# Scoring keys 16384 at a time in a decode attention kernel, with shared PE weights, longer DMA rows and a new split of the load buffers

## The chip, the cores and the metric

The kernel runs on one core of one Trainium2 chip. The time is device microseconds from launch to end, as the median of several executions. The span in a profile is counted from the first to the last instruction and is about 1.7 us shorter than the time. The profile names the engines PE (matmul), PEld (its weight loads), DVE (vector), ACT (scalar), POOL and SP (which issues the bulk loads). PEclk is the share of full speed that the PE clock is granted.

All runs used here are of the state that the measurement calls fast.

## The reference, cut to what matters

```python
def _A_ref(x, k_cache, v_cache, wq, wo):          # one token: attention over a cache
    q = (x @ wq)...                               # 32 heads of 128
    k = jnp.repeat(k_cache, 8, axis=1)            # 4 groups x 65536 keys x 128, bf16
    v = jnp.repeat(v_cache, 8, axis=1)
    p = _softmax(jnp.einsum('bhqd,bhkd->bhqk', q, k) * Dh ** (-0.5))
    return jnp.einsum('bhqk,bhkd->bhqd', p, v)... @ wo

def _B_ref(x, w_in, w_sp, b_sp, w_out):           # a gated mixer on the same token
    ...
return g * a + (1 - g) * b                        # g = sigmoid(sum(x * gate_w))
```

The two caches are 64 MB each (67.1 million bytes), the weights some 28 million bytes. In all 162.0 million bytes must be read from HBM for one token. There is little arithmetic per byte.

## The kernel before: the parts that matter

K and V come in pieces of 8192 keys, and one load brings a pair of them. The loads of K, V and the weights form one list, `stream`. SP issues the list in order on one queue, and load n goes to slot n % 5 of a ring of five slots of 32 KB per partition:

```python
NS = 5; SLOT = 16384                              # elements of 2 bytes
def kv(cache, n):                                 # two pieces: 32 KB per partition
    g, u = KV[n]
    return cache[0, g, UK * u:UK * (u + 2), :].rearrange("(p x) d -> p (x d)", p=128)

def issue(upto):
    while issued[0] < min(upto, len(stream)):
        n = issued[0]
        assert n < NS or all(k in used for k in stream[n - NS][0])
        ...
        P("SP", f, w=[("slot", s)], dma="s%d" % s)      # f: dma_start into slot n
```

A K piece is transposed by DVE in four quarters and scored by PE, four matmuls to a quarter, each with its own weights. Its scores are moved from PSUM by DVE (`score_piece`), exponentiated by ACT, transposed by DVE, and multiplied with V in four column groups of PE:

```python
def k_piece(n, j):
    ...
    P("DVE", lambda e: e.transpose(ktb(i).bitcast(F32), sl[:, 2048 * j:2048 * (j + 1)].bitcast(F32)), ...)
    def f(e):
        for fe in range(4):
            ...
            ins = e.matmul(pf(sb), qpad[g % 2][:, o:o + 128], vw(ktb(i), ...), ...)

def pv_piece(n):
    def f(e):
        for b in range(16):
            cg = b % 4
            ins = e.matmul(pf(OB)[32 * cg:32 * (cg + 1), :], ptsb(n)[:, 32 * b:32 * (b + 1)],
                           vw(sl, 128 * b, [[2048, 4], [1, 128]]), ..., tile_position=(0, 32 * cg), ...)
    P("PE", f, r=[("ptsb", n % 2), key], w=[B(OB)])
    done(("v", n))                                 # the slot may be loaded again
```

Of the kernel before, what the change touches and what calls it, by code (L numbers as in the profile page):

```python
# [137 lines left out]
def bass_gated_mix__gqa_block_cached__mixer_gmlp__decode_kernel(  # L138
# [25 lines left out]
    TILES = 64  # L164
    UK = 128 * TILES
    NU = Sk // UK
    NS = 5
    SLOT = 16384
    QP = 152
    NKTS = 3  # L170
    NSC = 10
    QW = DO // 4
    SCALE = 1.0 / math.sqrt(Dh)
# [3 lines left out]
    assert Sk % UK == 0 and FC == 14 and OC == 32 and HG == 8  # L177
# [4 lines left out]
    def region(name, nbf):  # L182
        nonlocal cur
        OFF[name] = cur
        cur += (nbf + 31) // 32 * 32

    for name, n in [
        ("RING", NS * SLOT), ("KT", NKTS * 2048), ("SC", NSC * 1024), ("PSB", 1024), ("PTSB", 1024),
        ("QPAD", 2 * 4 * QP), ("IDB", 128), ("IDF", 256), ("BM", 256), ("ONES", 256), ("SEL", 16 * 32),
        ("M16", 32), ("M8", 16), ("M32", 64), ("MQ", 32), ("OT", 256), ("XT", KC), ("WB", 2), ("WBB", 4), ("ONEB", 128), ("MAXC", 2 * G * NU), ("LP", 2 * G * NU),  # L190
        ("COLS", 2 * 64), ("DM", 32), ("QT", 32), ("QALL", 128), ("XW", 3 * KC), ("OSC", 512), ("OV", OC), ("Z", 2 * 28), ("Z2", 2 * 28),
        ("ZG", 2 * 28), ("ZE", 2 * 28), ("YB", FC), ("BROW", 2 * QW), ("OROW", QW),
    ]:
        region(name, n)
# [14 lines left out]
    idb, idf, bm, ones = ab("IDB", 128), af("IDF", 128), af("BM", 128), af("ONES", 128)  # L209
    sel, m16, m8 = ab("SEL", 512), af("M16", 16), af("M8", 8)  # L210
    m32, mq, ot = af("M32", 32), af("MQ", 16), af("OT", 128)
    xT, wb, wbb, oneb = ab("XT", KC), ab("WB", 2), af("WBB", 2), ab("ONEB", 128)
    qpad = [ab("QPAD", 4 * QP, 4 * QP * i) for i in range(2)]
    qall = ab("QALL", 128)
    maxc, lp, colt = af("MAXC", G * NU), af("LP", G * NU), af("COLS", 64)
    zc, z2, zg, ze = af("Z", 28), af("Z2", 28), af("ZG", 28), af("ZE", 28)
    yb, ovec, orow, brow = ab("YB", FC), ab("OV", OC), ab("OROW", QW), af("BROW", QW)
    osc, dm = ab("OSC", 512), af("DM", 16)
    qsb, qT, xw = ab("PSB", 512), ab("QT", 32), ab("XW", 3 * KC)
# [4 lines left out]
    def gcol(g, i):  # L224
        return col(C_G4 + 11 * g + i)

    (K_M, K_NB, K_MH, K_L, K_RL, K_F) = range(6)

    def slot(n):
        return ab("RING", SLOT, (n % NS) * SLOT)  # L230

    ktb = lambda i: ab("KT", 2048, (i % NKTS) * 2048)
    scs = lambda n: af("SC", 512, (n % NSC) * 512)
    psb = lambda i: ab("PSB", 512, 512 * (i % 2))
    ptsb = lambda i: ab("PTSB", 512, 512 * (i % 2))

    bank = [nc.alloc_psum_tensor("pb%d" % i, [128, 512], F32) for i in range(8)]
    FB, PTB, OB, MB = 0, 5, 6, 7
    SCB = [3, 4]
    pf = lambda i: bank[i][:, :]  # L240
    pbf = lambda i: bank[i][:, :].bitcast(BF16)
# [4 lines left out]
    def B(i):  # L246
        return ("bank", i)


    P("POOL", lambda e: e.memset(idf, 0.0), w=["idf"])  # L250
# [3 lines left out]
    for i in range(2):  # L254
        P("POOL", lambda e, i=i: e.memset(qpad[i], 0.0), w=[("qpad", i)])
# [3 lines left out]
    P("DVE", lambda e: e.memset(pf(MB), 0.0), w=[B(MB)])  # L259
    P("DVE", lambda e: e.memset(pf(OB), 0.0), w=[B(OB)])  # L260
    P("DVE", lambda e: e.memset(pf(FB), 0.0), w=[B(FB)])
    P("DVE", lambda e: e.memset(xw, 0.0), w=["xw"])
# [9 lines left out]
    xrow, grow, prod = ab("SC", 512, (NSC - 2) * 1024), ab("SC", 512, (NSC - 3) * 1024), af("SC", 512, (NSC - 4) * 512)  # L272
    KX, KG, KP = [("sc", NSC - i) for i in (2, 3, 4)]
# [10 lines left out]
    def load(keys, pieces):  # L284

        for i, key in enumerate(keys):
            place[key] = (len(stream), i)
        stream.append((keys, pieces))
# [4 lines left out]

    WQ_N = HQ * Dh

    def kv(cache, n):

        g, u = KV[n]
        return cache[0, g, UK * u:UK * (u + 2), :].rearrange("(p x) d -> p (x d)", p=128)

    def pair(name, cache, n):
        load([(name, n), (name, n + 1)], [(0, kv(cache, n))])

    KV = [(g, u) for g in range(G) for u in range(NU)]
    total = G * NU
    for i in range(0, 4, 2):
        load([("wq", i), ("wq", i + 1)], [(0, rows(A_wq, i // 2, 4))])
    steps = []
    for n in range(NU):
        if n % 2 == 0:  # L310
            pair("k", A_k_cache, n)
        aux = ()
        if n in (1, 3):
            load([("win", n - 1), ("win", n)], [(0, rows(B_w_in, n // 2, 4))])
            aux = (("win", n - 1), ("win", n))
        elif n == 5:
            load([("wout", 0), ("wout", 1)], [(0, rows(B_w_out, 0, 14))])
        elif n == 6:
            aux = (("wout", 0), ("wout", 1))
        steps.append((n, None, aux))  # L320
    for n in range(NU, total + NU + 1):
        k = n if n < total else None
        v = n - NU - 1
        if k is not None and k % 2 == 0:
            pair("k", A_k_cache, k)
        if v >= 0:
            if v % 2 == 0:
                pair("v", A_v_cache, v)
        else:
            v = None  # L330
        steps.append((k, v, ()))
    WO = [(0, 0, 8), (1, 0, 8), (2, 0, 8), (3, 0, 4), (3, 4, 6), (3, 6, 8)]
    for i, c0, c1 in WO:
        load([("wo", i, c0)], [(0, rows(A_wo, i, 8)[:, DO * c0:DO * c1])])

    WIDTH = {"wq": 2 * WQ_N, "win": 2 * F, "wout": 7 * DO, "wo": 8 * DO, "k": UK, "v": UK}
    issued = [0]
    used = set()

    def issue(upto):  # L340
        while issued[0] < min(upto, len(stream)):
            n = issued[0]
            assert n < NS or all(k in used for k in stream[n - NS][0])
            keys, pieces = stream[n]
            s = n % NS

            def f(e, n=n, pieces=pieces):
                for c0, src in pieces:
                    ins = e.dma_start(slot(n)[:, c0:c0 + src.shape[1]], src)  # L349
                return ins  # L350
            P("SP", f, w=[("slot", s)], dma="s%d" % s)
            issued[0] += 1

    def use(key):
        n, i = place[key]
        issue(n + 1)
        used.add(key)
        w = WIDTH[key[0]]
        return slot(n)[:, i * w:(i + 1) * w], ("slot", n % NS)

    def done(key):

        n = place[key][0]
        if key == stream[n][0][-1]:
            issue(n + NS + 1)

    issue(NS)
# [9 lines left out]
    P("DVE", lambda e: e.tensor_reduce(mq, vw(idf, 0, [[1, 16], [16, 8]]), AXX, ALU.add), r=["idf"], w=["mq"])  # L377


    sele = ab("SC", 512, (NSC - 1) * 1024)  # L380
    KSE = ("sc", NSC - 1)
# [5 lines left out]

    def f(e):
        for c in range(4):
            ins = e.transpose(pbf(PTB)[:, 2 * c:2 * c + 2], vw(xrow, c, [[4, 128]], 0, 2), idb[0:2, 0:2])  # L390
        return ins
    P("PE", f, r=[KX, "idb"], w=[B(PTB)])
    P("DVE", lambda e: e.tensor_copy(vw(xT, 0, [[4, 2], [1, 4]]), vw(pbf(PTB), 0, [[1, 2], [2, 4]])),
      w=["xT", B(PTB)])
    P("DVE", lambda e: e.tensor_copy(vw(xw, 1, [[3, KC]]), xT), r=["xT"], w=["xw"])
    P("PE", lambda e: e.matmul(pf(MB)[:, 0:2], oneb[0:1, :], wb[0:1, :], start=True, stop=True),  # L396
      r=["oneb", "wsp", "bsp"], w=[B(MB)])
    P("DVE", lambda e: e.tensor_copy(wbb, pf(MB)[:, 0:2]), w=["wbb", B(MB)])  # L398
# [4 lines left out]
    P("PE", lambda e: e.matmul(pf(PTB)[:, 0:1], ones[0:2, :], col(C_GS)[0:2, :], start=True, stop=True),  # L403
      r=["ones", "gs"], w=[B(PTB)])
    P("ACT", lambda e: e.activation(col(C_GE), pf(PTB)[:, 0:1], ACTF.Exp, scale=-1.0), w=["ge", B(PTB)])
# [5 lines left out]
    for i in range(4):  # L411
        sl, key = use(("wq", i))

        def f(e, i=i, sl=sl):
            for k in range(2):
                c = 2 * i + k
                for s in range(2):
                    for cg in range(4):
                        ins = e.matmul(pf(OB)[32 * cg:32 * cg + 2, :], xw[:, 3 * c + 1 - s:3 * c + 3 - s],  # L419
                                       sl[:, WQ_N * k + 512 * (4 * s + cg):WQ_N * k + 512 * (4 * s + cg + 1)],  # L420
                                       start=(c == 0 and s == 0), stop=(c == KC - 1 and s == 1),
                                       tile_position=(0, 32 * cg), skip_group_check=True)
            return ins
        P("PE", f, r=["xw", key], w=[B(OB)])
        done(("wq", i))
# [19 lines left out]



    nbatch = [0]
    pend = []

    def q_piece(g):
# [238 lines left out]
```

## Time and profile before

| | before |
|---|---|
| time | 386.56 us, median of 3 (386.56 to 386.72) |
| load queue busy, share of 16 engines' span | 98.2% |
| PE, DVE busy | 61%, 55% |
| 32 KB packet, median | 1.216 us, which is 16 x 32768 B / 1.216 us = 431 GB/s |
| last load byte | 381.2 us of a 384.9 us span |

From the page of the kernel before come the busy shares, two of the rows over 40 slices of the span (digits are tenths), the load queue (packets, MB, share of 16 engines), the chain of waits, and three groups of instructions (busy us, mean ns, then the idle time before them and what ended it):

```profile
span 384.9 us, 3607 instructions
PE 233.6 (61%) x1547; PEld 86.2 (22%) x1547; DVE 211.6 (55%) x329; ACT 30.6 (8%) x71; POOL 2.1 (1%) x9
...
PEclk9985969569996969696889696956796979866655
DMA  8999999999999999999999999999999999999994
...
q1 hardware_dynamic: 6200, 162.01, 98.2%
...
DMA 71%; PE 16%; DVE 11%; issue 0%; SPq 0%
...
L464 DVE STREAM_TRANSPOSE arena<-arena 128x1024 f32<-128x1024 f32 x128 | 151.4, 1217 | 75.3 <-DMA arena<-in_A_k_cache_dram 75.0
L472 PEld LDWEIGHTS pb<-arena 128*128 128x128 bf16 x512 | 46.7, 109 | 201.3 <-DVE arena L464 144.9
L516 PE MATMUL pb<-arena 128*32 128x512 bf16 x512 | 39.3, 441 | 20.6 <-DMA arena<-in_A_v_cache_dram 18.1
```

The DMA row has a 9 in every slice but the first and the last, so the loads bound the kernel from end to end. DVE waits 75.0 us for K, and PE 18.1 us for V. The weight loads of the scores (L472 PEld) are 46.7 us of work, but PEld waits 144.9 us for DVE before them, so they are not what PE waits for. The PEclk row alternates between 9 and 5 or 6: PE keeps falling idle, and after that runs at half clock for a while (below, after 6.11 us idle).

The timeline of the kernel before has 16 PV matmuls of one piece at full clock, and the last two pieces (32 matmuls) at half clock. Its columns are start us, length us, then the instruction:

```profile
186.41 1.05 PE L516 MATMUL pb<-arena 128*32 128x512 bf16 x16
...
362.18 3.60 PE L516 MATMUL pb<-arena 128*32 128x512 bf16 x32 [6.11 <-DMA arena<-in_A_v_cache_dram]
```

### The profile page before, as it was taken

What the parts mean: (1) busy time and instruction counts of PE and PEld (TensorE: products, weight loads), DVE (VectorE), ACT (ScalarE), POOL (GpSimd) and SP (SyncE); (2) the same over time, 40 slices, a digit from 0 to 9 for tenths busy, and PEclk for the clock granted to TensorE, in tenths of its full rate; (3) what the DMA queues carried; (4) which work ended last, traced back from release to release, by engine and by line L of the source; (5) the groups of instructions that cost most, each with busy time, mean ns of one, the idle gap of its engine ahead of it and who ended that gap; (6) DMA issues with size and microseconds to landing.
All of it is one profiled execution on the core that took longest, in us unless ns stands there. A gap on an engine that the chain in (4) does not pass through costs nothing.

```text
span 384.9 us, 3607 instructions
## 1 busy us (share of the span) xinstructions
PE 233.6 (61%) x1547; PEld 86.2 (22%) x1547; DVE 211.6 (55%) x329; ACT 30.6 (8%) x71; POOL 2.1 (1%) x9
## 2 busy tenths in 40 slices
PE   0434888478776656563687574726983829533354
PEld 0111455423221111111222121212220202211121
DVE  4115454489967474655596656645974748511010
ACT  1000000100300000001010000000100000320000
POOL 2000000000000000000000000000000000000000
PEclk9985969569996969696889696956796979866655
DMA  8999999999999999999999999999999999999994
GB/s 331 436 433 440 430 424 437 429 435 433 427 433 426 427 433 429 433 432 436 433 429 436 424 429 436 429 431 430 433 433 431 433 430 429 434 433 422 421 418 169
DMA packets 6228, 162.24 MB, mean 422 GB/s; under 512 B 700, under 2 KB 708, under 8 KB 964
## 3 DMA queue, kind: packets, MB, share of 16 engines
q1 hardware_dynamic: 6200, 162.01, 98.2%
q8 instruction: 12, 0.20, 0.2%
q14 instruction: 4, 0.03, 0.0%
q10 hardware_dynamic: 12, 0.00, 0.0%
HBM read 162.01 MB, written 0.00 MB: 421 GB/s over the span
## 4 chain that ended last, share of the span: by engine, by line
DMA 71%; PE 16%; DVE 11%; issue 0%; SPq 0%
DMA arena<-in_A_k_cache_dram 59%; PE pb L472 11%; DMA arena<-in_A_v_cache_dram 10%; DVE arena L464 9%; DMA arena<-in_A_wo_dram 3%; PE pb L516 2%; PE pb L558 2%; DVE arena L485 1%; PE pb L650 1%; DVE arena L507 0%; DVE arena L533 0%; PE pb L538 0%; PE pb L528 0%; SPq L349 0%; PE pb L495 0%
## 5 line engine op out<-in xcount | busy, mean ns | idle before, releaser
L472 PE MATMUL pb<-arena 128*128 128x512 bf16 x512 | 160.0, 457 | 93.6 <-DVE arena L464 91.7
L464 DVE STREAM_TRANSPOSE arena<-arena 128x1024 f32<-128x1024 f32 x128 | 151.4, 1217 | 75.3 <-DMA arena<-in_A_k_cache_dram 75.0
L472 PEld LDWEIGHTS pb<-arena 128*128 128x128 bf16 x512 | 46.7, 109 | 201.3 <-DVE arena L464 144.9
L516 PE MATMUL pb<-arena 128*32 128x512 bf16 x512 | 39.3, 441 | 20.6 <-DMA arena<-in_A_v_cache_dram 18.1
L502 ACT ACTIVATE arena<-arena 128x512 bf16<-128x512 f32 x32 | 23.1, 720 | 224.0 <-DVE arena L507 171.1
L507 DVE STREAM_TRANSPOSE arena<-arena 128x512 bf16<-128x512 bf16 x32 | 21.6, 679 | 18.5 <-PE pb L516 18.5
L485 DVE TENSOR_SCALAR_CACHE_REDUCE arena<-pb 128x512 f32<-128x512 f32 x32 | 21.6, 674 | 8.1 <-PE pb L472 7.9
L516 PEld LDWEIGHTS pb<-arena 128*32 128x32 bf16 x512 | 12.8, 106 | 45.0 <-issue 37.1
L558 PEld LDWEIGHTS pb<-arena 128*128 128x128 bf16 x224 | 13.8, 161 | 0.4
L558 PE MATMUL pb<-arena 128*128 128x1 bf16 x224 | 13.7, 198 | 0.0
L650 PE MATMUL pb<-arena 128*1 128x256 bf16 x128 | 7.8, 410 | 6.3 <-DMA arena<-in_A_wo_dram 6.3
L530 DVE RECIPROCAL arena<-pb 128x1 f32<-128x1 f32 x4 | 0.7, 168 | 18.4 <-PE pb L528 18.4
L419 PE MATMUL pb<-arena 128*2 128x512 bf16 x64 | 6.8, 601 | 4.2 <-DMA arena<-in_A_wq_dram 4.2
L656 DVE TENSOR_TENSOR arena<-pb,arena 97x256 bf16<-97x256 f32 x1 | 0.4, 425 | 13.4 <-PE pb L650 13.4
L396 PE MATMUL pb<-arena 1*128 1x2 bf16 x1 | 0.2, 158 | 10.1 <-DMA arena<-in_B_b_sp_dram 10.1
L426 DVE CAST arena<-pb 98x512 bf16<-98x512 f32 x1 | 0.7, 692 | 10.2 <-PE pb L419 10.2
L502 ACT ACTIVATION_READ_ACCUMULATOR arena<-arena 128x1 f32 x32 | 6.0, 187 | 0.0
L650 PEld LDWEIGHTS pb<-arena 128*1 128x1 bf16 x128 | 3.4, 109 | 10.5 <-DMA arena<-in_A_wo_dram 7.6
L538 PE MATMUL pb<-arena 128*128 128x128 bf16 x16 | 1.8, 243 | 5.2 <-DVE arena L533 5.2
L573 ACT ACTIVATE arena<-arena 128x28 f32<-128x28 f32 x1 | 0.2, 227 | 55.8 <-DVE arena L572 55.8
L569 DVE COPY arena<-pb 128x28 f32<-128x28 f32 x1 | 0.2, 186 | 7.8 <-PE pb L558 7.8
L398 DVE COPY arena<-pb 128x2 f32<-128x2 f32 x1 | 0.2, 159 | 7.7 <-PE pb L396 7.7
(88 smaller groups left out, 50.4 us busy)
## 6 DMA issues: line engine op xcount, KB each, us to landing
arena<-in_A_k_cache_dram SPq DMA_DIRECT2D x16, 4096.0 KB, 30.9
arena<-in_A_v_cache_dram SPq DMA_DIRECT2D x16, 4096.0 KB, 36.4
arena<-in_A_wq_dram SPq DMA_DIRECT2D x2, 4096.0 KB, 17.2
arena<-in_B_w_in_dram SPq DMA_DIRECT2D x2, 3584.0 KB, 40.9
arena<-in_A_wo_dram SPq DMA_DIRECT2D x3, 2048.0 KB, 34.9
arena<-in_B_w_out_dram SPq DMA_DIRECT2D x1, 3584.0 KB, 34.4
arena<-in_A_wo_dram SPq DMA_DIRECT2D x1, 1024.0 KB, 23.1
arena<-in_A_wo_dram SPq DMA_DIRECT2D x2, 512.0 KB, 13.1
```

Source lines behind the costliest of these rows:

```text
L419: ins = e.matmul(pf(OB)[32 * cg:32 * cg + 2, :], xw[:, 3 * c + 1 - s:3 * c + 3 - s], sl[:, WQ_N * k + 512 * (4 * s + cg):WQ_N * k + 512 * ...
L426: P("DVE", lambda e: e.tensor_copy(qsb[0:98, :], pf(OB)[0:98, :]), w=[("psb", 0), B(OB)])
L464: P("DVE", lambda e: e.transpose(ktb(i).bitcast(F32), sl[:, 2048 * j:2048 * (j + 1)].bitcast(F32)), r=[key], w=[("kt", i % NKTS)])
L472: ins = e.matmul(pf(sb), qpad[g % 2][:, o:o + 128], vw(ktb(i), 64 * f2 + ev, [[128, 16], [2, 32]]), start=(j == 0 and fe == 0), stop=(j == ...
L485: P("DVE", lambda e: e.tensor_scalar(scs(n), pf(sb), 0.0, None, op0=ALU.add, op1=ALU.max, accum_out=maxc[:, n:n + 1]), w=[("sc", n % NSC), ...
L502: P("ACT", lambda e: e.activation(psb(n), scs(n), ACTF.Exp, bias=gcol(g, K_NB), scale=SCALE, accum_out=lp[:, n:n + 1]), r=[("sc", n % NSC) ...
L507: P("DVE", lambda e: e.transpose(ptsb(n), psb(n)), r=[("psb", n % 2)], w=[("ptsb", n % 2)])
L516: ins = e.matmul(pf(OB)[32 * cg:32 * (cg + 1), :], ptsb(n)[:, 32 * b:32 * (b + 1)], vw(sl, 128 * b, [[2048, 4], [1, 128]]), start=(u == 0 ...
L530: P("DVE", lambda e: e.reciprocal(gcol(g, K_RL), pf(MB)[:, 0:1]), w=[("rl", g), B(MB)])
L538: ins = e.matmul(pf(MB)[:, 0:128], sel[:, 128 * c:128 * (c + 1)], osc[:, 128 * c:128 * (c + 1)], start=(c == 0), stop=(c == 3))
L558: ins = e.matmul(pf(MB)[:, z:z + 1], vw(sl, c0, [[FC, 128]]), xT[:, 2 * i + k:2 * i + k + 1], start=(i == 0 and k == 0 and z == 0), stop=( ...
L650: ins = e.matmul(pf(FB)[32 * q:32 * q + 1, 0:QW], ovec[:, 8 * i + c:8 * i + c + 1], sl[:, o:o + QW], start=(i == 0 and c == 0), stop=(i == ...
```

## The change

Its intent is fewer and larger DVE instructions, half the PE weight loads, and longer DMA rows. K is scored 16384 keys at a time, and two matmuls share one weight load. V pairs, wq and w_in come in rows of 64, 64 and 56 KB per partition. The 160 KB of load buffer are cut anew: three slots of 32 KB for K (`KR = 3`), and one area of 64 KB (`VB`) that V pairs, wq and w_in use one after another. The core of the diff, with cuts:

```diff
-    NS = 5
-    SLOT = 16384
+    SUB = 16384
+    KR = 3
+    NSUB = KR + 2
...
+    def mm(e, loaded, *a, **kw):
+        if not loaded:
+            return e.matmul(*a, **kw)
+        ...                                   # the same matmul with ldweights=False
...
+    VB = KR * SUB
+    def load_k(n):
+        load([("k", n)], kv(A_k_cache, n), kring())
+    def load_v2(n):
+        load([("v", n), ("v", n + 1)], kv(A_v_cache, n, True), VB)
+    load([("wq", 0)], rows(A_wq, 0, 8), VB)
+    load_k(0)
+    load_k(1)
+    load([("win", 0)], rows(B_w_in, 0, 8), VB)
+    load_k(2)
+    load_k(3)
+    load([("wout", 0)], rows(B_w_out, 0, 14), kring())
+    for i in range(6):
+        load_k(2 * i + 4)
+        load_v2(2 * i)
+        load_k(2 * i + 5)
+    load_v2(12)
+    load([("v", 14)], kv(A_v_cache, 14), kring())
+    load([("v", 15)], kv(A_v_cache, 15), kring())
+    for i in range(3):
+        load([("wo", i, 0)], rows(A_wo, i, 8), VB + 8 * DO * i)
...
+            for x in gr:                      # grains of 4 KB that this load covers
+                owner[x] = keys               # all its pieces must be used before the next load
...
     def pv_piece(n):
-            for b in range(16):
-                cg = b % 4
-                ins = e.matmul(pf(OB)[32 * cg:32 * (cg + 1), :], ptsb(n)[:, 32 * b:32 * (b + 1)],
...
+            for i in range(16):
+                b, t, cg = i // 8, 2 * (i % 8), i % 2
+                for h in range(2):
+                    ins = mm(e, h > 0, ob[64 * cg:64 * (cg + 1), 512 * h:512 * (h + 1)],
+                                   ptsb(n)[:, 512 * b + 32 * t:512 * b + 32 * t + 64],
+                                   vw(sl, 128 * (16 * b + t + h), [[4096, 4], [1, 128]]), ...
+                                   tile_position=(0, 64 * cg), skip_group_check=True)
```

PV now loads 64 columns of weights (two key tiles) and streams two V tiles past them. Half of each product is not wanted and is masked away later.

## The prediction

> **What bounds the kernel now.** DMA. The page's DMA line is 8-9 tenths in every slice but the last; the load queue is busy 98.2% of the 384.9 us span (queue table). In the trace a 32 KB packet takes 1.216 us (431 GB/s over 16 engines), 16 KB 0.613, 8 KB 0.312, 4 KB 0.159: about 10 ns plus 27.2 bytes per ns, and 16 x 27.2 = 435 GB/s, the fabric ceiling in the Trainium skill, "DMA: Bandwidth & Descriptors", Specifications. Packets run from 1.7 to 381.2 us with 378 us of packet time per engine: about 1.5 us of gaps, then 3.6 us of tail. The chain of waits agrees (DMA 71%). PE (61%) and DVE (55%) wait for data.
>
> **What the change does.**
> - Bytes: the same 162 MB. Rows of V, wq and win become 56-64 KB: some 1150 packets fewer x 10 ns / 16 = 0.7 us saved, if a packet can hold 64 KB.
> - PE: the same 512 score and 512 PV matmuls, half the weight loads (46.7 + 12.8 us now, overlapped). PV goes from four column groups at once (16 matmuls in 1.05 us) to two: a pair of PV pieces takes 33 x 0.216 = 7.1 us at full clock, 9-10.5 us if the first 3.4-6.8 us run at half clock, against 2.1-3.6 us.
> - DVE: the same transposes (151 us) in 64 pieces of 2.4 us; about 8 us less of evictions and P transposes.
> - Buffers: five 32 KB slots become three K slots and one 64 KB area for V pairs, single buffered. The queue is in order, so a V pair waiting for its area stops all behind it.
>
> The PE and DVE savings are off the critical path; what counts is whether the queue runs dry.
>
> **Where it can** (4 MB takes 9.7 us):
> 1. Near 85 us: K4 waits for the transposes of K2, which stand behind win, the mixer chain (6.2 us now, about 8 after) and a cold PE. I estimate K2 released at 85.5 and the queue empty at 86: stall 0-3 us, about 0.6.
> 2. Steady state: two K loads (19.4 us) lie between V pairs; PV needs 7-10.5, landing and issue about 2.5: no stall.
> 3. The last V pair (pieces 12, 13): only one K load lies before it. PV 7-10.5 + 2.5 - 9.7 = 0-3 us, about 1.5.
> The tail (wo in the same six loads) is unchanged.
>
> **Prediction.** 386.56 - 0.7 + 0.6 + 1.5, less some hope that stalls are hidden: 387.5 us, 80% range 385.0 to 392.0. Faster by over 2% (below 378.8) would nearly beat the packet time itself: 1%. Within 2%: 88%. Slower by over 2%: 11%.
>
> **What would show it.** Packets of 65536 bytes near 2.42 us; 430-436 GB/s in all slices but those near 86 us and 315-325 us; the queue's own waits on PV (before the last V pair) and on K transposes; weight loads halved; a pair of PV pieces 7-10.5 us.
>
> **What would make it wrong.** If the two 64-column groups don't overlap, a PV pair takes 14-20 us and every V load stalls: 395-405 us. Half clock after PE idles (the Trainium skill, "TensorE: Matmul & The Clock Gate", The HAM clock gate; here the first 5 us of a burst run at 427 ns per matmul) could stretch both stalls. If 64 KB rows slow HBM reads, all moves. If both stalls hide, 385.

## The result, and the profile after

The changed kernel takes 389.11 us (median of 4, 388.85 to 390.59), the kernel before 386.64 us in the same rounds. The ratio is 1.0071 with a 95% interval of 1.0054 to 1.0089: 0.7% slower, which is within 2%. A ratio here is the mean time of one kernel's fast runs over that of the other's of the same rounds, so it is not quite the ratio of the medians.

The same lines from the page of the changed kernel:

```profile
span 387.3 us, 2502 instructions
PE 232.9 (60%) x1367; PEld 56.0 (14%) x777; DVE 212.1 (55%) x229; ACT 25.8 (7%) x42; POOL 1.5 (0%) x8
...
PEclk9997998689997999689898997996989969969695
DMA  8999999999999999999999999999999998999994
...
q1 hardware_dynamic: 4904, 162.01, 97.5%
...
DMA 72%; PE 18%; DVE 7%; ACT 1%; issue 1%; SPq 0%
...
L481 DVE STREAM_TRANSPOSE arena<-arena 128x2048 f32<-128x2048 f32 x64 | 145.2, 2292 | 84.9 <-DMA arena<-in_A_k_cache_dram 78.8
L253 PE MATMUL obt<-arena 128*64 128x512 bf16 (+2 forms) x334 | 70.9, 449 | 44.5 <-DMA arena<-in_A_v_cache_dram 33.3
L253 PEld LDWEIGHTS scp<-arena 128*128 128x128 bf16 x256 | 26.1, 102 | 170.5 <-DVE arena L481 96.0
```

Nearly a third of the instructions (31%) is gone, and the weight loads of the scores went from 46.7 to 26.1 us, but PE and DVE are as busy as before. (L253 and L255 are the two lines of the helper `mm`: a matmul with its own weights, and one that uses weights already loaded.) What is new is one 8 in the DMA row, in the 34th slice, near 320 us. The windows view puts it more sharply. For three stretches it gives the busy time of each engine, then PEclk, the busy share of the DMA engines and GB/s; a packet is booked where it starts, so a share can pass 1. First the kernel before, then the changed one:

```profile
310.00:318.00 8.00, 3.30 (x8) 0.84 (x8) 4.60 (x6) 0.82 (x2) 0.00 (x0) 0.65 0.99 426
318.00:322.00 4.00, 4.00 (x28) 1.39 (x28) 3.73 (x6) 0.00 (x0) 0.00 (x0) 0.84 0.95 410
322.00:326.00 4.00, 3.24 (x14) 0.97 (x13) 3.33 (x4) 0.00 (x0) 0.00 (x0) 1.00 1.06 459
```

```profile
310.00:318.00 8.00, 5.80 (x36) 1.39 (x20) 0.00 (x0) 0.00 (x0) 0.00 (x0) 0.60 1.02 438
318.00:322.00 4.00, 3.71 (x34) 1.07 (x16) 0.14 (x1) 0.00 (x0) 0.00 (x0) 1.00 0.25 107
322.00:326.00 4.00, 1.77 (x8) 0.38 (x4) 3.93 (x6) 0.00 (x0) 0.00 (x0) 1.00 1.36 524
```

From 318 to 322 us the DMA engines were given 107 GB/s of work instead of 410. The timeline of the changed kernel around that gap shows the cause:

```profile
305.98 0.38 PE L255 MATMUL scp<-arena 128*128 128x512 bf16 x1
...
312.20 0.64 PE L253 MATMUL obt<-arena 128*64 128x512 bf16 x2 [5.84 <-DMA arena<-in_A_v_cache_dram]
...
316.47 0.39 PE L253 MATMUL obt<-arena 128*64 128x512 bf16 x2
...
321.01 0.38 PE L255 MATMUL obt<-arena 128*64 128x512 bf16 x2
...
321.43 1.28 SPq L371 DMA_DIRECT2D arena<-in_A_v_cache_dram  x3
```

PE ends the scores of K 14, then waits 5.84 us for V pieces 10 and 11. Its clock is at half when they land (a matmul's start comes 0.43 us after the last) and comes back at 316.5 us. PV of the two pieces runs from 312.20 to 321.4 us. Only then may SP issue the next V pair, into the same 64 KB; 14 and 15 go out in the same breath, because they had waited behind it in the queue. Everything that was queued before it (one K load of 9.7 us) was read by 319.0 us on the first DMA engine and 321.4 us on the last.

To put numbers on it I summed the packet records of the trace: the packet time of all engines divided by 16, and the idle time (16 minus the packets in flight, integrated, divided by 16) in each stretch. All are in us. The rows don't add up exactly, since two packets of one engine can overlap a little in the records.

| | before | changed |
|---|---|---|
| first packet starts | 1.74 | 1.76 |
| packet time per engine | 377.49 | 377.47 |
| idle, 80 to 90 us | 0.00 | 0.11 |
| idle, 310 to 326 us | 0.00 | 2.83 |
| idle after 370 us, to the last load byte | 1.95 | 1.63 |
| last load byte | 381.24 | 383.78 |
| from there to the end of the span | 3.63 | 3.53 |

The last load byte comes 2.54 us later, and the gap of 2.83 us is by far the largest new item. A second cost hides in the packet time: the median 64 KB packet took 2.419 us, but the first packet of each engine after the gap took 3.03 us on average. That is 0.6 us per engine for starting again. So the saving from the longer rows doesn't show in the sum.

### The profile page after: what moved, and what is told of

It is laid out like the page before. It is cut to its first block, busy times and chain, and to the rows that moved or that the text cites. A ratio compares the mean times of both kernels' runs of the same rounds, so it can differ in the third digit from the quotient of the medians.

```text
span 387.3 us, 2502 instructions
## 1 busy us (share of the span) xinstructions
PE 232.9 (60%) x1367; PEld 56.0 (14%) x777; DVE 212.1 (55%) x229; ACT 25.8 (7%) x42; POOL 1.5 (0%) x8
## 4 chain that ended last, share of the span: by engine, by line
DMA 72%; PE 18%; DVE 7%; ACT 1%; issue 1%; SPq 0%
DMA arena<-in_A_v_cache_dram 40%; DMA arena<-in_A_k_cache_dram 11%; DMA arena<-in_B_w_in_dram 8%; PE obt L253 8%; DMA arena<-in_A_wo_dram 8%; PE obt L255 8%; DMA arena<-in_A_wq_dram 6%; DVE arena L481 3%; PE scp L253 1%; PE scp L255 1%; DVE arena L519 1%; ACT arena L514 1%; SPq L371 0%; DVE arena L498 0%; DVE arena L595 0%
## 5 line engine op out<-in xcount | busy, mean ns | idle before, releaser
L481 DVE STREAM_TRANSPOSE arena<-arena 128x2048 f32<-128x2048 f32 x64 | 145.2, 2292 | 84.9 <-DMA arena<-in_A_k_cache_dram 78.8
L253 PE MATMUL scp<-arena 128*128 128x512 bf16 x256 | 105.9, 414 | 69.3 <-DVE arena L481 60.5
L255 PE MATMUL scp<-arena 128*128 128x512 bf16 x256 | 104.9, 410 | 0.0
L253 PE MATMUL obt<-arena 128*64 128x512 bf16 (+2 forms) x334 | 70.9, 449 | 44.5 <-DMA arena<-in_A_v_cache_dram 33.3
L255 PE MATMUL obt<-arena 128*64 128x512 bf16 (+2 forms) x334 | 70.0, 442 | 0.0
L253 PEld LDWEIGHTS scp<-arena 128*128 128x128 bf16 x256 | 26.1, 102 | 170.5 <-DVE arena L481 96.0
L253 PEld LDWEIGHTS obt<-arena 128*64 128x64 bf16 (+1 forms) x334 | 20.4, 120 | 108.4 <-issue 63.7
L514 ACT ACTIVATE arena<-arena 128x1024 bf16<-128x1024 f32 x16 | 18.4, 1148 | 226.5 <-DVE arena L510 113.7
L519 DVE STREAM_TRANSPOSE arena<-arena 128x1024 bf16<-128x1024 bf16 x16 | 19.4, 1213 | 10.6 <-PE obt L255 8.0
L498 DVE TENSOR_SCALAR_CACHE_REDUCE arena<-scp 128x1024 f32<-128x1024 f32 x16 | 19.3, 1205 | 9.3 <-PE scp L255 9.3
L704 PE MATMUL fbt<-arena 128*1 128x256 bf16 x128 | 6.2, 340 | 6.0 <-DMA arena<-in_A_wo_dram 6.0
L704 PEld LDWEIGHTS fbt<-arena 128*1 128x1 bf16 x128 | 2.9, 93 | 9.0 <-DMA arena<-in_A_wo_dram 6.9
```

The lines of the kernel that those rows point to most:

```text
L253: return e.matmul(*a, **kw)
L255: one = e.matmul(*a, **kw).ins
L481: P("DVE", lambda e: e.transpose(ktb(i).bitcast(F32), sl[:, 4096 * p:4096 * (p + 1)].bitcast(F32)), r=keys[2 * p:2 * p + 2], w=[("kt", i % ...
L498: P("DVE", lambda e: e.tensor_scalar(scs(n), sc_ps(n), 0.0, None, op0=ALU.add, op1=ALU.max, accum_out=maxc[:, n:n + 1]), w=[("sc", n % NSC ...
L514: P("ACT", lambda e: e.activation(psb, scs(n), ACTF.Exp, bias=gcol(n // NP, K_NB), scale=SCALE, accum_out=lp[:, n:n + 1]), r=[("sc", n % N ...
L519: P("DVE", lambda e: e.transpose(ptsb(n), psb), r=["psb"], w=[("ptsb", n % 2)])
```

## The experiments

The theory (A): the last V pair has only one K load ahead of it. PV of the pair before it, with the clock cold, takes longer than that load, and the queue is in order and runs dry. The rival (B): the loss is spread over the run, from the K rows that now have gaps between them, from 64 KB rows, or from the longer PV at the end. A rival for the size (A2): the gap is landing and issue latency, not PV.

| run | what is different | median us (range, runs) | ratio to before, 95% | idle 310-326 us | idle 80-90 us | packet time |
|---|---|---|---|---|---|---|
| changed | | 389.11 (388.85-390.59, 4) | 1.0071, 1.0054-1.0089 | 2.83 | 0.11 | 377.47 |
| e1_order | last loads reordered | 384.87 (384.72-388.15, 6) | 0.9975, 0.9948-1.0002 | 0.00 | 0.25 | 376.77 |
| e1b_order | the same, again | 385.35 (384.66-385.89, 5) | 0.9967, 0.9953-0.9981 | 0.00 | 0.18 | 376.82 |
| e2_halves | last V pair released by halves | 385.47 (384.88-387.50, 6) | 0.9981, 0.9961-1.0001 | 0.29 | 0.69 | 377.35 |
| e3_warm | PE kept warm before the PV pair | 386.77 (386.18-387.57, 6) | 1.0001, 0.9989-1.0013 | 0.71 | 0.04 | 377.31 |
| e4_pv4 | PV in four groups again | 386.39 (386.03-386.86, 5) | 0.9992, 0.9980-1.0004 | 0.41 | 0.39 | 377.53 |
| e5_rows32 | e1 with V in 32 KB rows | 385.43 (384.98-385.87, 5) | 0.9971, 0.9958-0.9983 | 0.00 | 0.22 | 377.48 |
| e6_reload | weights loaded for every matmul | 389.27 (389.13-390.26, 5) | 1.0076, 1.0063-1.0088 | 2.71 | 0.19 | 377.60 |
| e7_mixwarm | e1, and PE kept warm in the mixer | 384.73 (384.52-384.87, 5) | 0.9951, 0.9939-0.9964 | 0.00 | 0.08 | 376.53 |

The kernel before had medians of 386.63 us (with e1_order to e4_pv4) and 386.60 us (with the others). The changed kernel itself was timed in other rounds, with the kernel before (386.64 us) alone. e1_order to e4_pv4 ran on one chip, the others on a second, so compare runs of the two groups by their ratios. All ratios lie within 2% of 1; what is called faster or slower below rests on the interval. Each trace is of one run of its kernel, not always a typical one. All experiments gave correct results.

### e1_order and e1b_order: another load before the last V pair

```diff
+    load([("v", 14)], kv(A_v_cache, 14), kring())
     load_v2(12)
-    load([("v", 14)], kv(A_v_cache, 14), kring())
     load([("v", 15)], kv(A_v_cache, 15), kring())
-    for i in range(3):
-        load([("wo", i, 0)], rows(A_wo, i, 8), VB + 8 * DO * i)
-    s3 = kring()
+    s1 = kring()
+    for i in range(2):
+        load([("wo", i, 0)], rows(A_wo, i, 8), s1 + 8 * DO * i)
+    load([("wo", 2, 0)], rows(A_wo, 2, 8), VB)
+    s3 = VB + 8 * DO
```

> The changed kernel with only the order of its last loads altered: V piece 14 (a K slot that is long free) goes between K 15 and the V pair 12/13, and wo 0 and 1 take a K slot so that wo need not wait for that pair. Theory A (one K load, 9.7 us, is too little cover for 9.2 us of PV plus landing and issue, so the in-order queue runs dry at 318-322 us): the 2.8 us gap vanishes, and with it the 0.65 us by which the first packets after the dry spell took longer (3.1 instead of 2.42 us); time 389.1 - 3.4 = 385.7 us, within 385.2 to 386.3. Rival B (the loss is spread: strided K rows, 64 KB rows or longer PV at the end): the time stays at 388.5 to 389.5.

The first profile of this kernel fell on a run with an odd clock: where the other profiles have 1.00 and 0.50, it has 0.65 and 0.50. Its row:

```profile
PEclk9985665566666666566566665665666656655665
```

That run took 388.15 us, with PE late even after the last load; four of the other five took 384.72 to 384.96 us, one 387.14. So I ran it again for a usable trace:

> The same kernel as e1_order once more, because its profiled run was one with a granted clock of 0.65 while its other runs had 0.86 to 0.88. Theory A: most runs at 384.7 to 385.0 us, the profile without a gap at 318-322 us and with 376.8 us of packet time per engine; up to 0.7 us of gap near 86 us, where K 4 waits for the transposes of K 2.

The windows of e1b_order, as above:

```profile
310.00:318.00 8.00, 6.21 (x40) 1.58 (x22) 0.00 (x0) 0.00 (x0) 0.00 (x0) 0.64 0.93 401
318.00:322.00 4.00, 3.11 (x28) 0.86 (x12) 0.52 (x1) 0.00 (x0) 0.00 (x0) 1.00 1.09 467
322.00:326.00 4.00, 1.91 (x8) 0.38 (x4) 3.93 (x6) 0.00 (x0) 0.00 (x0) 1.00 1.03 442
```

The gap is gone though PV of the pair still begins at half clock (PEclk 0.64 in the first stretch), and the packet time fell by 0.65 us. Rival B is ruled out as the cause of the loss: the K rows, the 64 KB rows and PV are the same as in the changed kernel, and this kernel is 0.3% faster than before (0.9967, interval below 1). The edit did one thing more: wo went into other buffers and was issued from 326.7 us on instead of 348.9. Of the 4.2 us between the spans (387.3 and 383.1 us) the gap is 2.83 us and the packet time 0.65; 0.80 us is idle time after 370 us, which fell from 1.63 to 0.83. It stays at 1.60 to 1.85 us in e2_halves, e3_warm and e4_pv4, which leave wo as it was, and is 0.83 to 1.15 us in e1b_order, e5_rows32 and e7_mixwarm, which share this edit. So this part comes with the edit but not from the gap; why is not shown. The first median, 384.87 us, lay a little under the range that I had given (385.2 to 386.3), and my range for single runs of the second was too narrow: only two of the five runs lay at 384.7 to 385.0 us, the others between 385.35 and 385.89.

### e2_halves: the same order, a finer release

```diff
-    load_v2(12)
+    load([("v", 12)], kv(A_v_cache, 12), VB)
+    load([("v", 13)], kv(A_v_cache, 13), VB + SUB)
...
-            for x in gr:
-                owner[x] = keys
+            for j, x in enumerate(gr):
+                owner[x] = [keys[j * len(keys) // len(gr)]]
```

> The changed kernel, load order kept, but the last V pair comes as two loads of half the area, each released by its own PV piece. Theory A: piece 12 can be issued after one PV piece, about 5.5 us after the landing at 312.2 (half clock at first), that is at 317.8, just before the queue is dry at 319; no gap or under 0.5 us, 385.7 to 386.5 us. If the release of the whole area were not the cause (rival B), 388.5 to 389.5.

```profile
312.53 0.64 PE L253 MATMUL obt<-arena 128*64 128x512 bf16 x2 [5.21 <-DMA arena<-in_A_v_cache_dram]
...
318.40 0.38 PE L253 MATMUL obt<-arena 128*64 128x512 bf16 x2
...
319.04 4.75 SPq L372 DMA_DIRECT2D arena<-in_A_v_cache_dram  x4
```

The clock came back later here, at 318.3 us, so the first PV piece took 6.5 us. Piece 12 was still issued 2.4 us sooner than in the changed kernel, and the gap was 0.29 us. The median of 385.47 us is just below the range expected. (The trace is of the run that took 387.33 us, 1.9 us above the median. It holds 0.69 us of idle time near 86 us, to which I come under e7_mixwarm, and the 0.29 us here; the rest of its excess is not explained.) The gap follows the moment of the release, as theory A says. The order of the loads need not change if the area is released by halves.

### e3_warm: PE at full clock

```diff
+        if i == 5:
+            keep_warm(24)       # 24 matmuls of 512 columns into a bank that nothing reads yet
         pv_piece(2 * i)
         pv_piece(2 * i + 1)
```

> The changed kernel with 24 idle matmuls (512 columns, result thrown away) on PE between the scores of K 14 and the PV pair 10/11, so that PE is at full clock when V lands. Theory A1 (half clock made the PV pair 9.2 us rather than 7.0): PV pair 7.0 us, gap 2.8 - 2.2 = 0.6 us, restart cost maybe still paid; 386.3 to 387.2 us. Rival A2 (clock doesn't matter, landing skew and issue make the gap): PV pair stays at 9 us and the time at 388.5 to 389.5.

```profile
306.19 5.12 PE L669 MATMUL fbt<-arena 128*128 128x512 bf16 x23
...
311.77 0.41 PE L253 MATMUL obt<-arena 128*64 128x512 bf16 x2 [0.46 <-DMA arena<-in_A_v_cache_dram]
...
318.49 0.38 PE L255 MATMUL obt<-arena 128*64 128x512 bf16 x2
...
318.91 1.28 SPq L371 DMA_DIRECT2D arena<-in_A_v_cache_dram  x3
```

(The trace lacks one record of the 24.) With useless work in front of it, the PV pair took 7.1 us (311.77 to 318.9) instead of 9.2, and the gap fell from 2.83 to 0.71 us, that is by as much as PV. A2 is ruled out for this part. Half clock after an idle spell is what the Trainium skill, "TensorE: Matmul & The Clock Gate", Part 1, describes (half rate after an idle window of about 3.4 us). The trace of the changed kernel agrees: PE had been idle 5.84 us, and then ran at 0.427 us per matmul instead of 0.216 until 4.3 us into the burst. What remains of the gap at full clock is landing, issue and 7.1 us of PV against one 9.7 us load. The slow start was paid in full for this short gap too: the first packets took 3.03 us on average, and the packet time stayed at 377.31 us.

### e4_pv4: PV in four column groups again

```diff
-            for i in range(16):
-                b, t, cg = i // 8, 2 * (i % 8), i % 2
-                ...                              # two matmuls share 64 columns of weights
+            for i in range(32):
+                b, t, cg = i // 16, i % 16, i % 4
+                ins = e.matmul(ob[32 * cg:32 * (cg + 1), 0:512], ptsb(n)[:, 512 * b + 32 * t:512 * b + 32 * t + 32],
+                               vw(sl, 128 * (16 * b + t), [[4096, 4], [1, 128]]), ..., tile_position=(0, 32 * cg), ...)
```

(The eviction of the output, which then needs no mask, is put back with it.)

> The changed kernel with PV alone undone: 32 matmuls a piece in four column groups of 32, each with its own weights, as before the change, instead of pairs that share 64 columns of weights in two groups. Theory A: a PV pair takes 2 x 1.9 us at full clock, up to 5 us at half clock, so the area is released by 317.5 us, before the queue is dry at 319: no gap, 385.6 to 386.4 us although the order and the single V area stay. Rival B: 388.5 to 389.5.

```profile
312.96 5.97 PE L528 MATMUL obt<-arena 128*32 128x512 bf16 x64 [5.55 <-DMA arena<-in_A_v_cache_dram]
...
318.98 1.28 SPq L371 DMA_DIRECT2D arena<-in_A_v_cache_dram  x3
```

The time met the expectation at its upper end, the gap did not: 0.41 us remained. I had allowed 5 us for the pair at half clock. It took 6.0, since the clock came back only at 317.7 us, and V had landed 0.76 us later than in the changed kernel, after a dry spell of 0.39 us near 86 us. Shorter PV helps as theory A says, but it doesn't cure the cause.

### e5_rows32: what the long rows are worth

```diff
-        load([("v", n), ("v", n + 1)], kv(A_v_cache, n, True), VB)
+        load([("v", n)], kv(A_v_cache, n), VB)
+        load([("v", n + 1)], kv(A_v_cache, n + 1), VB + SUB)
```

> e1 with every V pair 0/1 to 12/13 loaded as two loads with 32 KB rows instead of one with 64 KB rows; same bytes, same places, same releases. If a packet costs a fixed 13 ns (2 x 1216 - 2419) beside its bytes, 896 more packets cost 896 x 13 / 16 = 0.7 us: packet time 377.5 us per engine and 385.4 us in time. Rival: the long rows do nothing, and the time is e1's 384.8.

The packet time is 377.48 us against 376.82 in e1b_order: 0.66 us, or 12 ns for each of the 896 packets, near the 13 expected. (The 13 was taken from the 32 KB packets of the kernel before and the 64 KB packets of the changed one; the medians of the changed kernel alone give 2 x 1.213 - 2.419, or 7 ns.) In the time it can't be seen: 385.43 against 385.35 us, with ranges that overlap. The releases are not the same, as I had expected: a load of one piece needs only its own half of the area, so here V is released by halves too. In the trace SP issues the two loads of the pair 2/3 at 116.64 us and some 5 us later, where e1b_order issues the whole pair at 126.61 us. An earlier issue could hide a loss from the short rows. The long rows save packet time, but this run doesn't show what that is worth in the end.

### e6_reload: shared weights undone

```diff
-        if not loaded:
+        if True:
             return e.matmul(*a, **kw)
```

> The changed kernel with one thing undone: every matmul loads its weights again (the sharing is gone; order, shapes and groups stay). If weight loads are off the path, as predicted, the time stays at 389.1, within 388.5 to 389.8, and the PV pair before the gap at 9 to 10 us; only the number of weight loads goes from 777 to 1367. Rival: shared weights shorten the PV pair that sets the gap; then the time is over 390 us.

```profile
PE 234.2 (60%) x1367; PEld 97.7 (25%) x1367; DVE 212.2 (55%) x229; ACT 25.8 (7%) x42; POOL 1.5 (0%) x8
```

PEld rises from 56.0 to 97.7 us, the PV pair takes 9.1 us as before, the gap is 2.71 us and the time 389.27. The shared weights, a good part of the change's work, are worth nothing here. They were off the path.

### e7_mixwarm: the other dry spell

The traces also show the first place that the prediction had named, near 86 us. K 4 waits for the transposes of K 2, those wait for PE to free a buffer, and PE is at half clock after the waits of the mixer chain. The timeline's issue of K 4 in the changed kernel, in e2_halves, and in e7_mixwarm:

```profile
84.31 0.33 SPq L371 DMA_DIRECT2D arena<-in_A_k_cache_dram  x1
```

```profile
85.79 0.33 SPq L372 DMA_DIRECT2D arena<-in_A_k_cache_dram  x1
```

```profile
82.90 0.33 SPq L373 DMA_DIRECT2D arena<-in_A_k_cache_dram  x1
```

The clock came back at 81.0 us in the first and 82.8 us in the second, and the idle time near 86 us was 0.11 and 0.69 us.

```diff
         done(("win", 0))
+        keep_warm(18)
...
+        keep_warm(14)
         P("DVE", lambda e: e.tensor_scalar(col(C_V), mb...
```

> e1 plus 18 and 14 idle matmuls on PE in the two waits of the mixer chain, so that PE is at full clock when the scores of K 2 begin. In the traces so far K 4 was issued at 83.6, 84.3, 85.3 and 85.8 us where the clock came back at 80.2, 81.0, 82.2 and 82.8 us, and the gap near 86 us was 0.04, 0.11, 0.39 and 0.69 us. Theory: K 4 issued near 82.7 us, no gap there, no runs at 387: all runs 384.3 to 384.9 us. Rival: the slower runs of e1 and e2 have another cause, and some stay at 387.

All five runs lie between 384.52 and 384.87 us. K 4 goes out at 82.90 us, and 0.08 us of idle time remain there. e1b_order, on the same chip and in the same rounds, spread from 384.66 to 385.89. So part of the spread between runs is probably this wait. The clock's return alone doesn't set it: the clock came back at 80.2 us in both e1b_order and e3_warm, but the transposes of K 2 began only at 74.94 us in the one and at 72.83 in the other, and K 4 went out at 85.17 and at 83.64 us. Nor does it explain every slow run: the 388.15 us run of e1_order was idle only 0.25 us here. Whether e7_mixwarm would be free of such runs stays open, as e1b_order had none in these rounds either. e7_mixwarm has the lowest median here, 0.9951 of the kernel before (0.9939 to 0.9964), but its interval overlaps that of e1b_order.

## Why the prediction was right or wrong, point by point

- **Bound by DMA, hence no gain from PE and DVE: right.** The changed kernel has a third fewer instructions and half the weight loads, and is not faster. e6_reload takes the shared weights back and costs nothing. The lighter DVE work that the prediction counted on doesn't show in DVE's busy time at all (211.6 and 212.1 us), and no run tests it.
- **387.5 us, range 385.0 to 392.0, within 2%: right.** The time was 389.11 us. The step that was mis-sized is the third place where the queue can run dry ("0-3 us, about 1.5"). It measured 2.83 us, and 2.71 in e6_reload. Of its terms, PV was in the stated range (9.2 of 7 to 10.5), but I used a middle value. "Landing and issue about 2.5" was really 3.3: the 16 DMA engines ended the V pair between 309.2 and 311.7 us (mean 310.1), PV began at 312.2, and from the end of PV at 321.4 to the first packets (mean 322.6) it took 1.2 us. The sum 2.1 + 9.2 + 1.2 - 9.7 is 2.8.
- **"Near 85 us ... stall 0-3 us, about 0.6": right in kind, rather large.** K 4 was issued at 84.31 us, not 85.5, and the stall was 0.11 us in the profiled run. It is 0.04 to 0.69 us over the other traces with the old mixer, and it moves with the end of the mixer chain and the clock's return.
- **"0.7 us saved" by longer rows: right in packet time, but not kept.** e1b_order and e5_rows32 differ by 0.66 us of packet time. In the changed kernel the sum was unchanged (377.47 against 377.49), because the packets after the gap took 0.6 us longer. I hadn't counted that a queue that ran dry also starts slowly.
- **"Some hope that stalls are hidden": wrong in the main.** Of the gap of 2.83 us, 2.54 us reached the last load byte.
- **"Steady state: no stall": right.** From 90 to 310 us the engines were idle 0.38 us in all, against 0.49 before.
- **"430-436 GB/s in all slices but those": a poor test.** A packet of 64 KB is booked where it starts, and the GB/s of a slice then swings between 393 and 476 though no engine waits. The busy share is the better column.
- **"If the two 64-column groups don't overlap, 14-20 us a pair": they do overlap.** e3_warm's pair of 64 matmuls took 7.1 us, which is 33 x 0.216. (The prediction's "against 2.1-3.6 us" is for a pair of the kernel before, which has half the keys. For as many keys that kernel needs 4 x 1.05 = 4.2 us at full clock.)

What stays open: the engines don't finish together at the end. The idle time after 370 us is 1.95 us before, 1.63 in the changed kernel and 0.83 in e1b_order, and I made no run that explains it. It is half of what e7_mixwarm gains over the kernel before. One run of e1_order at 387.14 us, one of e2_halves at 387.50, one of e6_reload at 390.26 and the 390.59 of the changed kernel have no trace.

## What to carry to other kernels

In a kernel bound by one in-order load queue, count for each load how many microseconds of loads are queued ahead of it, and compare that with landing, compute on the old content and issue, with PE at half clock; do it for the first and last turns of the loop too, where the order is another than in the middle. Merging two buffers into a larger one trades descriptor cost (here 0.66 us of packet time) against a later release (here 2.8 us of dry queue and 0.6 us of slow start). Here the cure was in the order of the list: one independent load moved ahead took the whole gap away.

## What the Trainium skill lacked or had wrong

- "TensorE: Matmul & The Clock Gate", Part 3, The mechanism, says that matmuls are strictly in order in start and end. In the query projection of the changed kernel each matmul is followed in program order by a partner on the same column group (L253, L255, L253, ...). In the trace four L253 start first, at 22.615 to 22.630 us (by the source, each in its own group; the trace doesn't name the group), then four L255 at 22.995 to 23.013. The 64 matmuls took about 5.5 us (22.61 to 28.06), which fits four at once, in part at half clock. If the instructions reached PE in the order of the source, matmuls of other groups went ahead of the partner that waited. The first lines of the timeline:

```profile
22.61 0.60 PE L253 MATMUL obt<-arena 128*1 128x512 bf16 x4 [0.15 <-DMA arena<-in_A_wq_dram]
23.00 0.65 PE L255 MATMUL obt<-arena 128*1 128x512 bf16 x4
23.42 0.65 PE L253 MATMUL obt<-arena 128*1 128x512 bf16 x4
```

- The same page, Part 1, names half and full clock, 13/16 when three cores of a die are busy, and a clock stuck at a quarter. In one profile of a program on one core (e1_order) the granted clock was 0.65 wherever the other profiles have 1.00.
- "DMA: Bandwidth & Descriptors", Latency and other measured facts, gives about 0.6 us to the first byte of a load issued by SP. Here the first packet of a load into a dry queue started 0.96 us after the issue (321.43 to 322.39), and the first packets took 3.03 us instead of 2.42.
- No page tells how far the 16 engines drift apart within one stream: at the end of a V pair the first was 2.5 us ahead of the last (309.16 and 311.69 us), and the landing waits for the last.
- "DMA: Bandwidth & Descriptors", Bandwidth, has about 10.5 ns a packet, from a 4 KB transfer of 64 packets, and gives no such figure for rows of 32 or 64 KB. Here they cost some 7 to 12 ns beside their bytes too: the medians in the changed kernel are 0.611, 1.213 and 2.419 us for 16, 32 and 64 KB, and 896 packets more cost e5_rows32 0.66 us on 16 engines.
